# Three constant products instead of seven, block 1 turned by VectorE and DMA instead of TensorE, and a new order of issue, in an adaLN block with linear attention and an MLP

## The chip, the core and the metric

The kernel runs on one core of a Trainium2 chip. A core has a matrix engine (TensorE, PE in the profile, with its weight loads as PEld), VectorE (DVE), ScalarE (ACT), GpSimd (POOL) and SyncE (SP, which here issues every DMA). Each engine takes its instructions strictly in the order in which the program issues them to it; engines wait for each other through semaphores. TensorE writes to PSUM, which has eight banks of 128 x 512 float32.

The metric is the device time of one execution in microseconds (us). Before the change it is 470.25, the median of three runs (469.98 to 470.39).

## What is computed

One token block of 2048 rows and 512 columns goes through an attention half and an MLP half, both modulated by a conditioning vector `c`:

```python
mod = (silu(c) @ w_mod).reshape(1, 6, 1, 512)          # sa, ca, ga, sb, cb, gb
h = layernorm(x) * (1 + ca) + sa
x = x + ga * A(h)                                      # linear attention
h = layernorm(x) * (1 + cb) + sb
x = x + gb * (gelu(layernorm(h) @ w1 + b1) @ w2 + b2)  # 512 -> 1376 -> 512

def A(h):                                              # 32 heads of 16
    q, k, v = split(h @ wqkv)
    pq, pk = q @ w_phi, k @ w_phi                      # per head, 16 x 16
    phi_q, phi_k = [concat(softmax(p), softmax(-p)) for p in (pq, pk)]
    kv, z = phi_k.T @ v, sum(phi_k)
    return (phi_q @ kv / (phi_q @ z + 1e-6)) @ wo
```

All arrays are float32.

## The kernel before

**Numbers and products.** A product of two float32 matrices is made of three products in a rounded format: each operand is split into a high part (a copy on ACT) and a low part (a subtraction on VectorE or POOL), and `mm3` (line 286) multiplies high by high, high by low and low by high. A tile of 128 rows against a 512 x 512 weight is therefore 12 products of 128x128 by 128x512.

**Phases.** The 2048 rows are eight blocks of 256, each with two tiles of 128 rows.

1. *Start.* `w_phi` is folded into the q and k weights: `fold_mm` (line 490) multiplies each of the four row pieces of `wqT` and `wkT` by a block-diagonal matrix `bd`, and `fold_out` splits the result into `wq` and `wk`. The modulation needs silu(c) spread over rows (`silu`, `silu_rows`, the scp products); `mod_cols` (line 372) reduces four loaded pieces `wm` against it to the columns of ca and sa, one piece for each 128 columns of x. `mod_rows` does the other four vectors later, piece by piece, in the background (`bg`, tile `wms`). Seven products of `ones` with itself (tile `warm`, lines 325 to 331) go to TensorE and are never read: four as item `init`, and one each as items `w2`, `w3` and `w4`.
2. *Blocks 0 to 7.* For each block: load x (tile `xt`), row statistics (`ln1_stats`, which ends in a small power on POOL, `rsa`), normalise in place (`ln1_apply`), turn the rows into columns, apply ca and sa (tile `hf`), split (`h_finish`, tile `hT`), then project: pk, pv and pq, each one tile of 12 products for each 128 rows. `k_chain` makes phi_k (on VectorE, ACT and POOL), `kv_mm` accumulates kv over all blocks. The q projections of blocks 3 to 7 are held back (`HOLD`) and fill TensorE later.
3. *The turn.* z and kv are summed up (`z_total`, `kv_blocks`) and the attention of blocks 0 and 1 is finished: t, o, w, la, lb, lc and y in the item names.
4. *Four MLP passes*, 0 to 3, each of 512 rows: `up` (u) and `down` (d), eleven column pieces each, between them the attention of the next two blocks, and the stores of the output (`mlp_out`).

**Turning rows into columns.** There are two ways in `ln1_apply` and `h_transpose`. For a block below `NT` (2 before, so blocks 0 and 1) TensorE transposes eight 128x128 pieces into PSUM (tile `hp`). For the others VectorE transposes 32x32 pieces into a tile `nb`, four DMAs store it to `nt_dram` in short pieces, and one DMA loads it back as `hd` with columns on the partitions. For block 0 `h_first` applies ca and sa and splits piece by piece, and `proj_first` runs its two pk tiles piece by piece (items `pf`), since its weights and modulation come in pieces too. The later blocks go through `hf`.

**The order of issue.** `Later` (line 220) collects every instruction of the program under an item and an engine, and `issue` (line 237) hands them out in the order of the lists in `ISSUE` (line 87), twelve parts: part 0 is the start and block 0, parts 1 to 6 are blocks 1 to 6, part 7 is block 7 and the turn, parts 8 to 11 are the four MLP passes. A word such as `fk.p` is the next instruction, or run of products, of item `fk` on TensorE (p; a is ACT, v VectorE, g POOL, s SP). A plus or minus in front takes it from a later or an earlier part. Item names: `db` loads the small constants, `x` an x block two ahead of the part's own, `dk`, `dq`, `dm`, `dv` the pieces of `wkT`, `wqT`, `wm` and `wv`; `fk`, `fq` fold, `ok`, `oq` split what was folded; `si`, `sr` are silu; `m` in part 0 is `mod_cols`; `s` and `n` are the statistics and the normalising with the turn (`s0`, `s1`, `n0`, `n1` those of blocks 0 and 1), `h` and `f` the way to `hT`; `vs` splits wv; `pk`, `pv`, `q` are projections, `k`, `v` the chains behind them, and `m0` to `m3` from part 1 on the kv products.

**Buffers.** Most tiles of the working set lie in 19 equal buffers; `SLOTS["buf"]` (line 46) names one for each tile in the order in which the program makes them, `SLOTS["bank"]` does so for the PSUM banks, and the other strings for small tiles. A tile waits for the last reader of what lay there before.

Of the kernel before, what the change touches and what calls it, by code (L numbers as in the profile page):

```python
# [15 lines left out]
P = 128  # L16
# [31 lines left out]
    "32eg91ai750d4gf6cf8ehcd187ga30203dh540b52ca0i999hba44571a6i7b8gag3fii0729f4c2fe569d1ehch8d61bg59801c"  # L48
    "7bda51ii68d72i6cc6g44bh676i1ia4e7ah24igi3g908053d78d90d850883efef7g7bbd7b5d5edbfe4id3f8g6f302hbab1ca"
    "gc1d035356268688c6ac633e1e6c0d3h2dffgahfi9f5df3d02gg340052aa2h0f05gc7532d6ggcbhd8g",  # L50
    "bank":
    "3534201077650761644611400766431302014372076341621740122107154521543753631407720101023324531207674567"
    "54567546767640763123523132153152524724605130311550313053514273015015610",
    "st6a": "11101010",
    "sta": "00010101",
    "vea": "01101101",
    "rsa": "01110001",
    "nma": "10111111",
    "dz": "001110010",
    "mxk": "1010101110101010",  # L60
    "smk": "0110010111011011",
    "rck": "1010010111101101",
    "mxq": "10110010",
    "smq": "00000000",
    "rcq": "10100020",
    "den": "00101110",
    "rd": "10111011",
    "st6b0": "10100110",
    "stb0": "10111101",
    "veb0": "10010101",  # L70
    "rsb0": "11001011",
    "st6c0": "01000110",
    "stc0": "10111100",
    "vec0": "00100100",
    "rsc0": "00101000",
    "nmc0": "10010111",
    "st6b1": "11110101",
    "stb1": "10000110",
    "veb1": "11111110",
    "rsb1": "00010101",  # L80
    "st6c1": "10000001",
    "stc1": "10111010",
    "vec1": "00110110",
    "rsc1": "00100101",
    "nmc1": "00000111",
# [3 lines left out]
-init.v -init.p dq.s db.s x0.s dk.s x1.s dk.s dm.s dk.s dm.s si.a bd.v dq.s fq.p s0.v -w2.p oq.a s0.v -w3.p si.v  # L89
-init.v s0.v dk.s s0.v si.v fk.p si.v s0.v dm.s s0.v oq.v s0.g sr.p s1.v n0.v n0.v s1.v n0.a fq.p s1.v n0.v ok.a  # L90
sr.a fk.p s1.v ok.v x.s m.g dm.s m.v h0.p dv.s ok.a fk.p s1.v bg.s s1.v m.v oq.a ok.v m.a m.g m.v h0.p ok.a -w4.p
f.v +x.s s1.g ok.v fq.p m.a n1.v f.a m.v fk.p n1.a f.v dv.s n1.v f.v m.g oq.a pf.p oq.v f.a n1.a f.v ++x.s m.v ok.a
pf.p m.a m.v oq.v m.g f.v h.p s.v f.a fq.p h.a m.v m.a h.p f.v pf.p bg.s h.a s.v +bg.s h.a s.v +bg.s s.v oq.a s.v
m.v s.v f.v s.g +++x.s oq.v f.a bg.g vs.a f.v q1.p n.v +s.v h.a ok.v vs.a n.v vs.v pf.p n.a vs.g ++s.v n.a q0.p k1.v
bg.a n.v n.v +bg.g bg.v n.s pv0.p +s.v n.s f.a +bg.g ++s.v q1.a n.s +bg.a +s.v ++s.v n.s k1.v f.g +bg.a +bg.s ++s.v
++s.v +s.v +s.v ++s.v k0.v f.a pv1.p k0.v f.g +++s.v n.s k1.v ++++x.s +bg.g +s.v k0.v k0.v
""",
    """
pk1.p s.g +s.g n.v n.v bg.v n.a bg.g -k1.v n.a bg.s ++++x.s ++s.v -q0.a +bg.s pk0.p bg.v -k1.a e.v h.a h.a ++s.v
++s.v n.v -k0.a q1.p +n.v bg.v -v1.a +bg.g ++s.v n.v bg.a e.v h.a n.s +n.a n.s -k0.v f.a pv0.p n.s -v0.a f.g n.s h.a  # L100
+bg.v f.a +++s.v e.g bg.a bg.v q0.p f.g k0.v +n.v +n.v +n.a e.g ++++s.v +bg.a +++s.v q1.a +bg.s
""",
    """
q0.p --k1.v -q0.a -n.s +s.v bg.v +s.g n.v bg.g --k0.v n.s -pv1.p -k1.v n.s --k1.v n.s +n.v e.v bg.g n.s -k1.v -e.g
pk0.p h.a --v1.v ++s.v bg.v h.a -e.g +n.v -k1.v bg.a --v0.v ++s.v --k0.g f.a -v1.v -k0.v h.a +++s.v q1.p -v1.a n.s
--v0.v -k0.v +n.a --v1.v --k1.g -k1.v bg.a -k0.v q0.a k0.v h.a pv0.p f.g -k1.a ++s.v bg.v -e.a -k1.v +n.a -m0.p f.a
-m1.p +n.v bg.p pk1.p k0.v bg.a -k0.a bg.s +++s.v ++s.v +n.v ++s.g +h.a v0.v f.g +n.s ++n.v v0.a -k1.v -k0.v +h.a
bg.s pv1.p +n.s -e.a e.g bg.s ++n.v e.v +h.a bg.s +n.s ++n.a +++s.v e.g bg.s +f.a +n.s v1.v
""",
    """  # L110
pk0.p h.a -k1.v --k1.g -bg.s -q1.a ++s.v ++s.v -k0.v +n.a -k1.v -v1.a --v0.v -k0.v -e.g pk1.p k0.v f.g -v0.v --v1.v
--k0.v --v0.v +n.v ++s.g +n.v --k0.g k0.v pv0.p +n.s ++n.v k0.v +n.s ++n.a k0.v +n.s f.a -e.g --e.v -q1.s -k0.a +n.s
# [25 lines left out]
o10.v la00.v o11.v +a0.g -bg.a la00.v la00.v la00.g w11.p +a0.g la01.v +a0.g w1.g lb00.v la01.a +a0.v la01.v lb00.v
w10.p la11.v w1.s q1.s la01.v lb00.v la11.a la01.v la01.v +lp1.s la01.g w2.s la11.v -bg.g lb01.v q3.p la11.v lb01.v
la10.v +a0.g lb01.v la11.v la10.a lb00.v lb01.v la11.v lb00.g lb01.g q3.p la10.v la11.g lc00.v la10.v lc01.v la10.v  # L140
lc01.a la10.v la10.g lb11.v +a0.g lc00.a lb10.v q3.a y0.p q3.a lb11.v y0.p y0.a +a0.g lb10.v q3.s y0.a y0.v --bg.a
lb10.v y0.v
""",
    """
u0.p -w1.a -lb11.v -lb10.v -lb11.v a0.v -lb10.g -lb11.g u0.p a0.v ---bg.g -lc10.v -lc11.v a0.v a0.s -lc10.a a1.v
a0.s u0.p -lc11.a a0.s a1.v a0.s a1.g -y1.p -y1.p -y1.a u0.p --v0.v a0.v a1.g -y1.a -y1.v a0.s a1.g -y1.v a1.a a0.s
u1.p a0.s a1.g a0.s u1.p -w1.g +lp0.s u.a u.a u1.p u.a u.v a0.s u.a a1.v a0.s -w2.g d.p -w1.s u.a d.p u.v u.a d.p
u.v d.p a1.g a1.a d.p d.p -w2.a a1.v d.p a1.g d.p a1.v d.p x0.s a1.v u1.p -w2.g a1.v o01.p o00.p +a0.v d.p o00.a
a1.g -w2.s o01.a o00.v d.p a1.g a1.g +a0.g u.p a1.v o01.v u.a a1.g a1.g d.p a1.g w01.p a1.v u.a +a0.v u.a -w1.a u.v
u.a -w2.g a1.v d.p la01.v a1.s d.p a1.v la01.a a1.s w00.p u.v +a0.g -w2.a a1.s a1.v a1.s -w2.g la01.v a1.s a1.s  # L150
+a0.a u.p a1.s la00.v a1.s la00.a -w1.g -w2.s la00.v la01.v +a0.g la01.v la00.v la00.v la00.v d.p u.a la01.g la01.v
a1.s d.p u.a a1.s +a0.g d.p u.v u.p lb01.v la00.g +a0.a lb00.v -w2.g lb01.v lb00.v lb00.v d.p lb01.v u.a lb01.v
lb00.v lb01.g d.p -w2.a lb00.g lc01.v u.p lc00.v +a0.v lc01.a -w2.g u.a lc00.a u.v y0.v d.p +a0.g u.a y0.v -w2.s
x1.s o10.p +a0.v -w2.s o11.p y0.s u.a d.p y0.s o10.a +a0.g o11.a y0.s d.p o10.v y0.s o11.v w10.p +a0.v +a0.v +a0.v
# [42 lines left out]
u.a u.a d.p u.a u.a u.a u.v d.p d.p d.p d.p d.p out.v d.p out.s d.p out.v d.p out.s d.p out.v d.p out.s out.v out.v  # L197
out.s out.s
""",
]  # L200
W2A = 6
AHEAD = 4
NT = 2
BUFS = 19
ALIGN = 64
NE = 2


class Held:
# [35 lines left out]
def adaln_hedgehog_mixer(ctx, tc, x, wqT, wkT, wv, wo, w1, w2, b2, wmodT, small_in, out):  # L245
    nc = Later(tc.nc)
# [52 lines left out]
    ones = consts.tile([P, 1], F32, name="ones")  # L299
# [16 lines left out]
    bd = wtile("bd", [4, 8, DH])  # L316
# [855 lines left out]
```

## Time and profile before

| | us |
|---|---|
| median of three runs | 470.25 |
| the profiled execution | 470.68 |
| its span in the profile, first to last instruction | 468.9 |
| TensorE busy | 462.5 |
| VectorE, ACT, POOL busy | 314.1, 235.6, 279.7 |

All times in the views count from the start of the span. "Busy" is the union of an engine's instructions; neighbouring instructions overlap at their ends by a little, so the price of a product is the distance between starts, not the duration of one. In the timeline a row stands for a run of like instructions (its start, its length, engine, source line, operation, output and inputs, shape, count). Every line reads L217 or the like, because `Later` issues all instructions from one place; a group is known by its tile names. The granted clock is 0.999 of full speed over the execution.

### The profile page before, as it was taken

Reading aid. Unit: us, or ns where it says so; the run is one execution under the profiler, and the core shown is the slowest. Engines: PE = TensorE matmul, PEld = TensorE weight load, DVE = VectorE, ACT = ScalarE, POOL = GpSimd, SP = SyncE. Lnnn points to the kernel's source line nnn. Section 1 sums busy time; section 2 is a strip of 40 time slices with the busy share of each in tenths; the row PEclk is TensorE's granted clock in tenths of the full one; section 3 lists DMA queues with packets and bytes.
Section 4 is the critical chain, followed back from the end, with each engine's and each line's share of the span. In section 5 each row is a group of like instructions: output and inputs, shape, how many; then the busy total and the mean of one; then the engine's idle time right before and its main releaser. Section 6 shows DMA issues by size and latency. Waiting matters only on the chain.

```text
span 468.9 us, 8567 instructions
## 1 busy us (share of the span) xinstructions
PE 462.5 (99%) x3313; PEld 375.2 (80%) x3313; DVE 314.1 (67%) x610; ACT 235.6 (50%) x383; POOL 279.7 (60%) x233
## 2 busy tenths in 40 slices
PE   9999999999999999999999999999999999999996
PEld 5888888888878878988787878788788788788884
DVE  4999989998848389578885869795873282211113
ACT  2777686855541555758537672166533224422221
POOL 0485859879899989999879975663740010400000
PEclk9999999999999999999999999999999999999999
DMA  8999639636622446937636838168337205100002
GB/s 293 401 263 296 148 78 244 220 65 217 205 64 89 141 174 228 223 112 163 191 97 135 223 113 202 48 110 196 118 76 178 87 0 135 46 22 24 0 1 89
DMA packets 81033, 67.00 MB, mean 143 GB/s; under 512 B 52560, under 2 KB 68320, under 8 KB 80736
## 3 DMA queue, kind: packets, MB, share of 16 engines
q1 hardware_dynamic: 80992, 66.46, 50.1%
q8 instruction: 26, 0.43, 0.4%
q14 instruction: 15, 0.12, 0.1%
HBM read 44.41 MB, written 22.03 MB: 142 GB/s over the span
## 4 chain that ended last, share of the span: by engine, by line
PE 92%; DVE 3%; issue 1%; ACT 1%; DMA 1%; DVEq 0%; ACTq 0%
PE pg L217 26%; PE py L217 26%; PE pv L217 9%; PE pk L217 9%; PE pq L217 7%; PE pw L217 7%; PE warm L217 2%; PE pkv L217 2%; PE fold L217 1%; DVE pw L217 1%; PE po L217 1%; DMA pq_dram<-qs 1%; ACT qT L217 1%; DVE st6c L217 1%; PE zp L217 0%
## 5 line engine op out<-in xcount | busy, mean ns | idle before, releaser
L217 PE MATMUL pg<-yT,w 128*128 128x512 f32 (+1 forms) x528 | 115.5, 370 | 0.7 <-DVE yT L217 0.4
L217 PEld LDWEIGHTS pg<-yT,w 128*128 128x128 f32 x528 | 92.9, 188 | 18.2 <-DVE yT L217 0.6
L217 ACT ACTIVATE pg<-pg,blob 128x512 f32<-128x512 f32 x44 | 29.1, 661 | 106.5 <-PE pg L217 104.3
L217 DVE TENSOR_TENSOR g<-pg,g 128x512 fp32r<-128x512 f32 x40 | 27.2, 684 | 66.9 <-ACT g L217 66.7
L217 PE MATMUL py<-w2a,g 128*128 128x512 f32 x288 | 71.9, 392 | 0.0
L217 PEld LDWEIGHTS py<-w2a,g 128*128 128x128 f32 x288 | 53.5, 188 | 13.4 <-issue 1.6
L217 PE MATMUL py<-w2b,g 128*128 128x512 f32 x192 | 47.2, 390 | 0.0
L217 PE MATMUL pv<-wvh,hT 128*128 128x512 f32 x192 | 45.8, 392 | 0.0
L217 PE MATMUL pk<-wk,hT 128*128 128x512 f32 x192 | 45.6, 391 | 0.0
L217 PE MATMUL pw<-wo,oT 128*128 128x512 f32 x192 | 45.6, 390 | 0.0
L217 PE MATMUL pq<-wq,hT 128*128 128x512 f32 x192 | 45.2, 390 | 0.0
L217 POOL TENSOR_TENSOR ez<-eq,zb 128x1024 f32<-128x1024 f32 x15 | 36.4, 2440 | 13.2 <-PE pg L217 6.1
L217 PEld LDWEIGHTS py<-w2b,g 128*128 128x128 f32 x192 | 35.9, 188 | 8.1 <-issue 0.7
L217 PEld LDWEIGHTS pw<-wo,oT 128*128 128x128 f32 x192 | 35.9, 188 | 7.8 <-issue 0.4
L217 PEld LDWEIGHTS pq<-wq,hT 128*128 128x128 f32 x192 | 35.9, 188 | 7.4
L217 PEld LDWEIGHTS pv<-wvh,hT 128*128 128x128 f32 x192 | 35.7, 188 | 7.5
L217 PEld LDWEIGHTS pk<-wk,hT 128*128 128x128 f32 x192 | 35.8, 188 | 7.3
L217 POOL TENSOR_TENSOR ek<-ek,rck 128x1024 f32<-128x1024 f32 x16 | 31.0, 1947 | 4.3 <-ACT vf L217 1.6
L217 POOL TENSOR_TENSOR eq<-eq,rcq 128x1024 f32<-128x1024 f32 x15 | 28.9, 1939 | 0.2
L217 ACT ACTIVATE g<-pg 128x512 fp32r<-128x512 f32 x40 | 24.0, 599 | 9.5 <-DVE stc L217 2.8
L217 POOL TENSOR_TENSOR rsb<-veb,mhalf 128x1 f32<-128x1 f32 x16 | 8.8, 550 | 30.3 <-DVE veb L217 30.3
L217 POOL TENSOR_TENSOR yT<-yf,yT 128x256 fp32r<-128x256 f32 x24 | 17.1, 744 | 15.2 <-ACT yT L217 15.2
(154 smaller groups left out, 802.4 us busy)
## 6 DMA issues: line engine op xcount, KB each, us to landing
et_dram<-eb SPq DMA_DIRECT2D x48, 128.0 KB, 2.8
eT<-et_dram SPq DMA_DIRECT2D x12, 512.0 KB, 5.5
xt<-in_x SPq DMA_DIRECT2D x8, 512.0 KB, 6.4
wms<-in_wmodT SPq DMA_DIRECT2D x8, 512.0 KB, 5.9
x<-in_x SPq DMA_DIRECT2D x8, 512.0 KB, 3.8
out<-x SPq DMA_DIRECT2D x15, 256.0 KB, 2.1
nt_dram<-nb SPq DMA_DIRECT2D x24, 128.0 KB, 3.3
hd<-nt_dram SPq DMA_DIRECT2D x6, 512.0 KB, 4.2
```

The source lines that it names most:

```text
L217: return lambda *a, **k: self.later.hold(self.letter, lambda: f(*a, **k))
```

## The change

The numbers of `ISSUE` and `SLOTS` are all new. Beside them two things are edited: the constant products are three, all in item `init`, and `NT` is 1, so that block 1 takes the way over `nb`, `nt_dram` and `hd`.

```diff
-    for name in ("init", "w2", "w3", "w4"):
-        nc.item(name)
-        for _ in range(4 if name == "init" else 1):
-            nc.tensor.matmul(warm, ones.to_broadcast([P, P]), ones.to_broadcast([P, 512]), start=True, stop=True)
-    nc.item("init")
+    for _ in range(3):
+        nc.tensor.matmul(warm, ones.to_broadcast([P, P]), ones.to_broadcast([P, 512]), start=True, stop=True)
...
-NT = 2
+NT = 1
...
 ISSUE = [
     """
--init.v -init.p dq.s db.s x0.s dk.s x1.s dk.s dm.s dk.s dm.s si.a bd.v dq.s fq.p s0.v -w2.p oq.a s0.v -w3.p si.v
--init.v s0.v dk.s s0.v si.v fk.p si.v s0.v dm.s s0.v oq.v s0.g sr.p s1.v n0.v n0.v s1.v n0.a fq.p s1.v n0.v ok.a
...
+-init.v -init.v -init.p db.s x0.s x1.s dk.s dq.s dm.s si.a si.v dk.s si.v bd.v si.v dk.s sr.p dq.s s0.v s0.v s0.v
+s0.v s0.v s0.v s0.g sr.a dm.s s1.v s1.v s1.v n0.v s1.v n0.v dm.s s1.v s1.v n0.v s1.g fk.p dm.s ok.a x.s fq.p n0.a
+ok.v fq.p oq.a n1.v n1.v m.v m.g n1.a h0.p dk.s oq.v fk.p m.v m.a n1.v ++x.s fk.p oq.a f.v ok.a oq.v fq.p n1.a ok.v
+fq.p f.a m.g m.v f.v h0.p m.v pf.p n1.v m.a m.g n1.s oq.a f.v ok.a dv.s m.v m.g f.a n1.s m.a f.v pf.p n1.s m.v m.v
+oq.a n1.s m.a f.v dv.s fk.p m.v ok.v f.a bg.s f.v +x.s pf.p oq.v f.v s.v f.a ok.a f.v vs.a oq.v q0.p s.v s.v s.v s.v
+ok.v n1.s q1.p bg.s s.v ++s.v s.g +bg.s vs.a vs.v vs.g n.v ++s.v n.a n.v pf.p n.a n.v n.v pv1.p bg.g ++s.v k0.v n.s
+h.a q0.a +s.v n.s h.a +s.v n.s q1.a +bg.g +s.v ++s.v n.s ++s.v k0.v f.a pv0.p ++++x.s h.a +bg.v f.g +bg.s h.a +s.v
+++s.v k0.v f.a +bg.s +s.v ++s.v +bg.s k1.v +s.g k1.v f.g
...
```

What the lists mean for one engine is seen best by taking its words alone. SP in part 0 (the first `n` four times are a block's stores, the fifth is its load `hd`; an @ and a number marks words of another part):

```text
before  dq db x0 dk x1 dk dm dk dm dq dk dm x dm dv bg x@1 dv x@2 bg bg@1 bg@1 x@3 n n n n bg@1 n x@4
after   db x0 x1 dk dq dm dk dk dq dm dm dm x dk x@2 n1 dv n1 n1 n1 dv bg x@1 n1 bg bg@1 n n n n x@4 bg@1 bg@1 bg@1
```

TensorE in parts 0 to 7, to the turn (the lists go on with t, o, w, q and y):

```text
before  0 init fq w2 w3 fk sr fq fk h0 fk h0 w4 fq fk pf pf h fq h pf q1 pf q0 pv0 pv1
        1 pk1 pk0 q1 pv0 q0
        2 q0 pv1@1 pk0 q1 pv0 m0@1 m1@1 bg pk1 pv1
        3 pk0 pk1 pv0
        4 pk1 pk0 m0@2 m1@2 m0@3 pv1@3 pv1
        5 pk0 pk1 pv0@4 m1@3 m0@4 m1@4 pv0 pv1
        6 pk1 pk0 m0@5 m1@5 m0 pv1
        7 pk1 pk0 m1@6 m1 pv0@6 pv0 pv1 q1 m0 m2 m3 z kf q0 q1 q2 q2 q0 q4 ...
after   0 init sr fk fq fq h0 fk fk fq fq h0 pf pf fk pf q0 q1 pf pv1 pv0
        1 pk1 pk0 q0 pv1 q1 pv0
        2 pk1 pv0 pv1 pk0 q1 m0@1 m1@1 bg q0
        3 pk1 pk0
        4 pk0 pk1 pv1 m0@2 m1@2 m0@3 pv0@3 pv0 pv1@3
        5 pk1 pk0 m1@3 m0@4 m1@4 pv0
        6 pk1 pk0 pv1@5
        7 pk1 m0@5 m1@5 m0@6 pv1@6 pk0 pv0 m1@6 m1 pv1 pv0@6 q1 m0 m2 m3 z kf q1 q2 q0 q2 q0 q4 ...
```

In parts 8 to 11 the products of `u` and `d` are the same and stand in another order among each other; of the stores and loads, the five of block 5's way back to columns (`y1`) move from part 9 to the start of part 10, and two stores of pass 2 move from the start of part 11 to its end, between those of pass 3.

More of the change, by code (lines that the diff above doesn't have):

```diff
@@ L82 @@
[L82 to L85, printed above, removed]
+    "1264710140570135353253136162435026621304533162143502472521023727652170445605353123554624602715375317"
+    "153573175304761253153253215213576546037217123132712723327513246406462",
+    "st6a": "01110010",
+    "sta": "01010101",
+    "vea": "10101001",
+    "rsa": "01110110",
+    "nma": "10001001",
+    "dz": "001001011",
+    "mxk": "1010100110011010",
+    "smk": "0100011001010101",
+    "rck": "0010011010101001",
@@ new lines @@
+    "mxq": "01011011",
+    "smq": "00000000",
+    "rcq": "02002110",
+    "den": "10000010",
+    "rd": "11010110",
+    "st6b0": "10111000",
+    "stb0": "01010111",
+    "veb0": "01100100",
+    "rsb0": "01110010",
+    "st6c0": "11010100",
+    "stc0": "11001000",
+    "vec0": "00110010",
+    "rsc0": "11011010",
+    "nmc0": "11110010",
+    "st6b1": "11110111",
+    "stb1": "00000011",
+    "veb1": "10111001",
+    "rsb1": "01101110",
+    "st6c1": "11100001",
+    "stc1": "01000010",
+    "vec1": "10100011",
@@ L86 @@
+    "rsc1": "01000111",
+    "nmc1": "11011001",
 }
@@ new lines @@
+n.s f.g -v1.v -v0.v +n.a k0.v k1.v -bg.g k1.v -pv1.p -k1.v n.s k0.v -bg.g +n.v k0.a +n.v
+""",
+    """
+pk1.p -k1.a --k1.v n.s -k0.v n.s --v0.a --k0.g --v1.a n.s ----e.v h.a n.s -bg.a pk0.p ----e.s --k1.g -k1.v h.a h.a
+-k0.v f.a n.s k1.v h.a -bg.g -bg.s --m1.p k0.v f.a -m0.p --v0.v -v1.v -m1.p +++lp0.s pv0.p v1.v -k1.v f.g k0.v k1.v
+f.g ----e.v k1.v
+""",
+    """
+pk1.p --k0.g h.a -k1.v -k0.v -k1.a --k1.g h.a -k1.v -v0.a pk0.p ----e.a -k0.v --bg.g f.a k1.v h.a -v0.v k1.v -k0.a
+---v1.v -pv1.p k0.v h.a -k0.v f.g f.a +w1.s --bg.a -k1.v f.g -k0.v --v0.a
@@ new lines @@
+d.p lb10.v d.p lb10.v d.p lb10.v lb11.v d.p lb10.g lb11.v lb11.v lc10.v d.p lb11.g lc10.a +a0.g lc11.v u.p lc11.a
+y1.v u.a y1.v +a1.v y1.s +a0.g y1.s +a1.v u.p u.a y1.s y1.s u.v yf0.a +a1.g yf0.g u.a d.p u.a +a1.g y1.s d.p +a0.v
+u.a d.p u.v yf0.a u.a d.p +a0.v yf0.g u.a u.a d.p ++a0.v u.a xb.g +a0.s d.p +a0.s yf0.a +a0.v yf0.a d.p +a0.s u.a
+u.v +a0.s d.p yf1.a +a0.v yf0.g yf1.a d.p yf1.a +a0.s yf0.g yf1.a d.p d.p +a0.s yf1.g d.p out.v d.p yf1.g +a1.a
+out.v d.p out.s yf1.g out.s +a1.v yf1.g
@@ new lines @@
+""",
+    """
+u.p a0.s a0.s a1.g -out.v a1.g u.p u.a a1.g u.a a0.s u.v a0.s x0.s -out.s a1.a d.p d.p a1.v a1.g d.p d.p u.a u.p u.a
+u.v a1.v a1.v d.p u.a a1.v d.p o00.p -out.v o01.p a1.g a1.g -out.s d.p o00.a a1.g +a0.g a1.v u.a d.p o01.a u.v a1.g
+u.p a1.g o01.v o00.v a1.g a1.v d.p u.a +a0.v d.p u.a w00.p a1.v +a0.g a1.v a1.s +a0.g +a0.a a1.s a1.s +a0.g w01.p
+a1.s la00.v +a0.a a1.v +a0.v a1.s a1.s la00.v d.p a1.s la00.v d.p a1.s +a0.v +lp1.s u.p x1.s la00.v u.v la00.v
+la01.v la00.g a1.s +a0.v a1.s +a0.g d.p u.a la00.v d.p u.a lb00.v d.p lb00.v +a0.g u.p u.v +a0.v la01.v d.p +a1.v
@@ new lines @@
+lb11.v u.a lb11.v u.a lb11.v lb11.v +a0.s lb11.g u.v +a0.s d.p xb.g u.a lb10.v lc11.v +a1.v d.p d.p lb10.v u.p
+lb10.g +a1.g lc10.v +a1.v u.a u.v d.p u.a y0.s d.p lc10.a d.p lc11.a y1.v d.p u.a y1.v u.a
+""",
+    """
+o01.p a1.v -y1.s -u.a -u.a o00.p -u.a -y1.s a1.g a1.v -d.p -y1.s -yf0.a -d.p -y1.s -yf0.a o01.a -d.p x0.s o00.a -d.p
+-u.a o00.v -d.p -u.v -y1.s -yf0.a -d.p o01.v a1.v -d.p -d.p -d.p -out.v -d.p a1.g -d.p -yf0.g -out.v -out.s w01.p
+-out.v a1.g -out.s a1.g -yf0.g a1.v -yf1.a -out.v -yf0.g -yf1.a -yf1.a -yf1.g -yf0.a w00.p -yf1.a -yf1.g -yf1.g a1.g
@@ new lines @@
+-yf1.g -yf0.g u.p a1.g a1.g u.p u.a u.a u.v la00.v a1.v d.p u.a la01.v u.p u.a la01.v a1.v u.v a1.s la01.v a1.s d.p
+u.a a1.v -out.s d.p u.a a1.s la01.v la01.v la01.v d.p la01.g -out.s la00.v a1.s d.p lb01.v d.p la00.v d.p la00.v
+a1.v u.p u.v a1.s la00.v lb01.v a1.s la00.g la00.v a1.s a1.s lb00.v d.p u.a lb01.v d.p u.a d.p u.v d.p lb00.v a1.s
+d.p lb00.v lb00.v lb01.v lb00.g d.p a1.s lb01.g lc00.v d.p lc01.v u.p u.p u.a lc00.a u.a lc01.a u.v y0.v d.p u.a
+y0.v o11.p u.a o10.p y0.s y0.s d.p o10.a o11.a y0.s o10.v d.p x1.s o11.v d.p y0.s d.p w10.p w11.p la10.v u.v y0.s
@@ new lines @@
+""",
+    """
+u.p u.p u.a u.a u.v -out.v -out.v d.p -out.s u.a d.p -out.s u.a -d.p d.p -out.v d.p u.v d.p u.p u.p u.a u.a u.v d.p
+u.a d.p u.a d.p u.v d.p d.p d.p d.p d.p d.p d.p d.p u.p -d.p u.a u.p -out.v u.a u.v d.p u.a d.p u.a d.p u.v d.p d.p
+u.p d.p u.a d.p u.a d.p u.v u.p d.p u.a d.p u.a d.p u.v d.p d.p d.p d.p u.p d.p u.a u.p u.a u.v u.p u.a u.a u.v d.p
+u.a d.p u.a d.p u.a u.a d.p u.a u.a u.a u.v d.p d.p d.p d.p out.v d.p out.s d.p out.v -out.s -out.s d.p out.s d.p
+out.v d.p out.s out.v out.v out.s out.s
```

172 lines of the change are left out of this document (54 added, 118 removed).

## Prediction

> **What bounds the kernel now.** I read the page's busy line and its chain of work first: is one engine the bound?
>
> ```profile
> PE 462.5 (99%) x3313; PEld 375.2 (80%) x3313; DVE 314.1 (67%) x610; ACT 235.6 (50%) x383; POOL 279.7 (60%) x233
> PE 92%; DVE 3%; issue 1%; ACT 1%; DMA 1%; DVEq 0%; ACTq 0%
> ```
>
> TensorE is busy 462.5 of 468.9 us, and 92% of the chain lies on it. Next I read what it waited for; these are all of its waits but the 0.9 us before its first product:
>
> ```profile
> PE zp L217 <- ACT kvT L217: 0.5, 1, 0.5
> PE pg L217 <- DVE yT L217: 0.4, 1, 0.4
> PE po L217 <- ACT qT L217: 0.4, 1, 0.4
> PE pg L217 <- ACT yT L217: 0.3, 1, 0.3
> ```
>
> Only 1.6 us in all. So there are two ways to a shorter time: take work off TensorE, or lose those waits. Any new wait of TensorE counts in full. Third, its timeline at the start, where the change takes work away (start, duration, operation):
>
> ```profile
> 0.92 6.67 PE L217 MATMUL warm<-ones 128*128 128x512 f32 x8 [0.92 <-DVE ones L217]
> 7.43 1.05 PE L217 MATMUL fold<-bd,q 128*128 128x128 f32 x8
> 8.31 1.89 PE L217 MATMUL warm<-ones 128*128 128x512 f32 x4
> 10.04 1.05 PE L217 MATMUL fold<-bd,k 128*128 128x128 f32 x8
> ...
> 15.68 1.03 PE L217 MATMUL warm<-ones 128*128 128x512 f32 x2
> 16.55 1.05 PE L217 MATMUL fold<-bd,q 128*128 128x128 f32 x8
> ...
> 21.09 0.60 PE L217 MATMUL hp<-blob,xt 128*128 128x128 f32 x4
> 21.52 1.06 PE L217 MATMUL fold<-bd,q 128*128 128x128 f32 x8
> 22.41 0.60 PE L217 MATMUL hp<-blob,xt 128*128 128x128 f32 x4
> ...
> 31.03 5.60 PE L217 MATMUL pv<-wvh,hT 128*128 128x512 f32 x24
> 36.47 5.60 PE L217 MATMUL pk<-wk,hT 128*128 128x512 f32 x24
> ```
>
> **What is removed.** Prices are differences of starts. w2 and w3: 10.04 - 8.31 = 1.73 us. w4: 16.55 - 15.68 = 0.87. Block 1's transposes through TensorE (the hp rows at 21.09 and 22.41): 21.52 - 21.09 = 0.43, twice, 0.86. The fourth product at the very start: a quarter of 7.43 - 0.92 = 6.51, so 1.63. Sum: **5.1 us** of TensorE work. That is a ceiling, since the products may only have filled a wait for data.
>
> **What is late next: the loads.** The new order of SP puts the fourth piece of wk (dk) behind three pieces of the modulation weights and x of block 2, the wv loads (dv) behind x of block 4 and block 1's four stores, and block 1's load hd behind those. So I work out landings from the rate of the transfers (the columns are the stretch, its length, busy time of TensorE, its weight loads, VectorE, ACT and POOL, the granted clock, the DMA's busy share, GB/s):
>
> ```profile
> 0.00:10.00 10.00, 9.08 (x20) 4.37 (x21) 3.47 (x14) 2.09 (x3) 0.91 (x5) 1.00 0.84 272
> 10.00:20.00 10.00, 9.91 (x75) 8.90 (x74) 8.94 (x29) 8.01 (x17) 5.43 (x5) 1.00 1.03 405
> 20.00:30.00 10.00, 10.00 (x54) 8.53 (x53) 9.59 (x24) 7.91 (x17) 5.19 (x4) 1.00 0.99 380
> 32.00:34.00 2.00, 2.00 (x11) 1.65 (x10) 2.00 (x11) 2.00 (x6) 2.00 (x2) 1.00 1.03 174
> ```
>
> The engines of the DMA are full from 10 to 30 us, so landing goes by bytes in the queue: 2.72 MB by 10 us, then 0.405 MB/us, from 20 us 0.38. A test on before: the last k piece, with 4.30 MB up to and with it, is served at 10 + 1.58/0.405 = 13.9; it landed at 6.81 + 8.2 = 15.0:
>
> ```profile
> 6.81 0.33 SPq L217 DMA_DIRECT2D k<-in_wkT  x1
> k<-in_wkT SPq DMA_DIRECT2D x1, 256.0 KB, 8.2
> ```
>
> So I add 1.1 us. Block 1's stores to nt_dram go in short pieces; while block 2's ran (last row of the windows) a full queue moved 174 GB/s in place of 380 to 405, so they count double. In the new order:
> - last k piece: 5.88 MB, 10 + 3.16/0.405 + 1.1 = **18.9** (before 15.0);
> - second half of wv: 8.50 MB counted; 6.77 are through by 20, so 20 + 1.73/0.38 + 1.1 = **25.7**;
> - hd of block 1: 10.07 MB, 20 + 3.30/0.38 + 1.1 = **29.8**.
>
> **TensorE's new start, gate by gate.** Three products end near 6.0. Silu's rows, seven folds, block 0's transposes and two of the four groups of the first pk (pf) follow as pieces land. The second of these groups wants the second modulation piece, which is at 4.04 MB: 10 + 1.32/0.405 + 1.1 = 14.4. Four or five VectorE steps of some 0.6 us (the transposes' row further down shows such a step) bring its rows to about 17.0, and a group takes 1.36 (a quarter of 36.47 - 31.03 = 5.44, for half as many products as a tile of 2.72), so 18.4; TensorE then waits 0.5 for the last k piece. From 18.9: one fold (8.31 - 7.43 = 0.9), pf 1.36, q0 and q1 2.72 each, pf 1.36: 9.1, so v starts at **28.0** against 31.03. Gate two: wv's second half needs a copy on ACT and a subtraction on POOL:
>
> ```profile
> 25.90 1.09 ACT L217 ACTIVATE wvh<-wv_s 128x1024 fp32r<-128x1024 f32 x1
> 27.06 3.19 POOL L217 TENSOR_TENSOR wvh<-wv_s,wvh 128x1024 fp32r<-128x1024 f32 x1 [1.52 <-ACT wvh L217]
> ```
>
> 25.7 + 1.0 + 3.2 = 29.9, needed 1.36 + 0.45 after v starts, at 29.8: a wait of 0.1 to 0.2. Two v tiles (5.44) end at **33.6**. Gate three: block 1's transposed rows.
>
> ```profile
> L217 ACT ACTIVATE hf<-hd,affine x8: 585/592/601, 40.4 to 59.4; 128x256 f32<-128x256 f32 x8
> L217 ACT ACTIVATE hT<-hf x5: 614/624/633, 31.1 to 56.1; 128x512 fp32r<-128x512 f32 x5
> L217 POOL TENSOR_TENSOR hT<-hf,hT x4: 1297/1301/1319, 32.7 to 47.6; 128x512 fp32r<-128x512 f32 x4
> ```
>
> From 29.8 ACT does hf, a q copy, hf, a q copy and the first hT: some 0.5 us apart, 32.0; POOL's 1.3 ends at 33.3. Two more hf, hT, and POOL with a small rs in between: 35.3. Wanted at 33.6 + 0.45 and 33.6 + 1.36 + 0.45 = 35.4. So all three gates nearly tie, and pk of block 1 starts at 33.6 against 36.47: **2.9 us earlier**; 2.2 of the 5.1 turn into waits for loads.
>
> **What is added beside it.** Two VectorE transposes (0.70 each), four stores and one load. VectorE has room where they fall, before 26 us, and none just after:
>
> ```profile
> L217 DVE STREAM_TRANSPOSE nb<-xt x12: 652/700/712, 29.1 to 99.6; 128x512 f32<-128x512 f32 x12
> 0.00:26.00 26.00, 24.99 (x128) 18.51 (x129) 18.00 (x58) 15.02 (x32) 8.59 (x12) 1.00 0.96 351
> 26.00:60.00 34.00, 34.00 (x151) 28.16 (x151) 33.14 (x83) 23.85 (x49) 26.24 (x21) 1.00 0.79 224
> ```
>
> I take 0; with that cover gone, VectorE's 1.4 us come late and cost up to 1.4. The second transpose waits on VectorE behind the reduction of the second modulation piece (about 14.4), so it ends near 16.4. SP stands at block 1's first store until then, with both wv loads queued behind; the transfers still have work until 20.3 (x of block 4 is the last in the queue), so I take 0 and keep 0 to 1.5. The fewer constant products cost nothing by themselves: at the start they run 1.63 each, later 0.87, so the array speeds up between; silu's rows keep it busy across that point (I keep 0 to 0.9, the folds at half pace, which lies ahead of the 18.9 gate).
>
> By the Trainium skill, "DMA: Bandwidth & Descriptors", Specifications, transfers in pieces under 512 B cost a read-modify-write, which speaks against a further block through DRAM in the fullest part of the queue; the 174 GB/s window agrees, and the sum above already pays it from that row. Were short pieces free, hd and the second half of wv would land 1.4 us sooner (0.52/0.38) and the sum would gain the 0.2 of the v gate; at a third of the rate it is rival B.
>
> **The rest of the order.** From 36.47 on the products are the same in number and kind; I take the 1.6 us of waits as they were (the same items stand around zp, po and the first pg in the new lists), and 0.3 for new small waits, between -1.6 and the rival below. At the end two stores of pass 2 go between the last ones on SP; they drain before the last product, so 0. Sum: 2.9 - 0.3 = **2.6 us**. The profiled execution took 470.68 (span 468.9 and 1.8 around it), so 468.1 there; against the median of 470.25: **467.6**.
>
> **Rivals.**
> (A) *A later block's rows come late, slower.* The new order defers v and m tiles, so block 7's first pk stands further ahead than the gain alone puts it. I add up the new list from 33.6 (26 tiles of 2.72 and eight kv tiles of 0.6, a third of the pkv row below, are 75.5): it starts at 109.1, where 117.5 - 2.9 would be 114.6. Before, and VectorE's busy time around it:
>
> ```profile
> 105.32 0.38 SPq L217 DMA_DIRECT2D hd<-nt_dram  x1
> 114.14 2.57 POOL L217 TENSOR_TENSOR hT<-hf,hT 128x512 fp32r<-128x512 f32 x2
> 112.88 1.85 PE L217 MATMUL pkv<-ek,vf 128*17 128x32 f32 x192
> 117.50 2.88 PE L217 MATMUL pk<-wk,hT 128*128 128x512 f32 x12
> 60.00:90.00 30.00, 30.00 (x439) 24.70 (x439) 26.81 (x56) 21.73 (x35) 23.96 (x18) 1.00 0.58 158
> 90.00:123.00 33.00, 33.00 (x513) 27.09 (x511) 30.12 (x55) 19.34 (x28) 28.53 (x17) 1.00 0.61 184
> ```
>
> From hd's issue to the end of hT: 116.7 - 105.3 = 11.4. The second half of hT is wanted 1.8 into the tile, at 110.9, so hd must be issued by 99.5. On SP it waits behind block 7's four stores, these on VectorE's transposes, and VectorE, full until 60, may be behind. If the chain keeps before's time, hT is done at 116.7, 5.8 late: 470.25 - 2.6 + 5.8 = **473.4**. It decides from 2.6 us late. For it: the tile is pulled 5.5 us beyond the gain. Against: VectorE waits 3.2 + 2.9 us between 60 and 123, and before ran its own tight order there without a wait of TensorE.
> (B) *The hd gate is late.* The stores share a full queue; if they are served at a third of the rate (1.4 us more) and SP stands 0.6 longer, hd lands 2 us later and pk of block 1 waits 2: **469.6**, no measurable change.
> (C) *The products were filler.* If the last k piece lands at 21 (SP held up by a buffer), everything from 28.0 shifts by 2.1: **469.7**. It would mean that the change does not do what it says: work goes, waits come.
> (D) *The remaining waits go too.* Loads 1 us sooner and half of the 1.6 us gone: about **465.7**.
>
> **How the numbers follow.** Forecast 0.62 (467.6; its own range 466.3 to 469.2), A 0.19, B 0.08, C 0.06, D 0.05. A measurement here tells a change from none at about 0.2%, 0.94 us. Faster: 0.62 + 0.05 = 0.67; the same: B and C, 0.14; slower: A, 0.19. The range takes D in below and the nearer part of A above: 465.3 to 471.3.
>
> **What would show it.** Right: 6 and not 14 passes of warm; no hp of block 1; pk's first row x24 of block 1 near 33.6; the last k piece landing near 19, hd near 30; TensorE idle some 2 us more in the first 20 us and busy throughout from 34 to 130. Wrong: a wait of TensorE on hT of POOL or ACT between 35 and 120 (A), a wait there of over 1 us just before 34 (B), TensorE idle over 2 us ahead of the last fold (C), or pass 2's products of pg waiting for yf, whose stores moved into the next part.

## The result, and the profile after

| | us |
|---|---|
| before, median of 12 runs | 470.21 (469.42 to 470.56) |
| after, median of 12 runs | 467.74 (466.95 to 469.86) |
| ratio, 95% interval | 0.9949 (0.9937 to 0.996) |
| after, the profiled execution and its span | 468.37, 466.6 |

The changed kernel is 2.5 us faster. Its runs spread over 2.9 us, those of before over 1.1. First the busy line of the page of the changed kernel:

```profile
PE 458.5 (98%) x3297; PEld 372.3 (80%) x3297; DVE 317.1 (68%) x612; ACT 234.6 (50%) x381; POOL 279.7 (60%) x233
```

TensorE's busy time fell by 4.0 us and the span by 2.3, so 1.7 us of what went came back as idle time. (By the starts 5.1 us were priced as removed; a busy row also holds short gaps between its instructions, so the two need not agree.) These are all waits of TensorE after (in total, times, longest):

```profile
PE warm L218 <- DVE mhalf L218: 0.9, 1, 0.9
PE fold L218 <- DMA k<-in_wkT: 0.9, 1, 0.9
PE pk L218 <- ACT hT L218: 0.7, 1, 0.7
PE zp L218 <- ACT kvT L218: 0.6, 1, 0.6
PE pg L218 <- DVE yT L218: 0.3, 1, 0.3
PE pg L218 <- ACT yT L218: 0.3, 1, 0.3
PE po L218 <- DMA eT<-et_dram: 0.2, 1, 0.2
PE pk L218 <- POOL hT L218: 0.2, 1, 0.2
```

The timeline of TensorE at the start shows where the first three fall (start, duration, operation, wait before it):

```profile
0.92 5.11 PE L218 MATMUL warm<-ones 128*128 128x512 f32 x6 [0.92 <-DVE mhalf L218]
5.86 1.05 PE L218 MATMUL scp<-blob,sc 128*128 128x128 f32 x8
7.78 1.16 PE L218 MATMUL fold<-bd,k 128*128 128x128 f32 x8 [0.86 <-DMA k<-in_wkT]
...
15.32 1.64 PE L218 MATMUL pk<-wk,hT 128*128 128x512 f32 x6
17.63 1.65 PE L218 MATMUL pk<-wk,hT 128*128 128x512 f32 x6 [0.68 <-ACT hT L218]
19.12 1.05 PE L218 MATMUL fold<-bd,k 128*128 128x128 f32 x8
...
28.20 5.60 PE L218 MATMUL pv<-wvh,hT 128*128 128x512 f32 x24
33.64 2.02 PE L218 MATMUL pk<-wk,hT 128*128 128x512 f32 x8
35.82 3.94 PE L218 MATMUL pk<-wk,hT 128*128 128x512 f32 x16 [0.17 <-POOL hT L218]
39.60 0.62 PE L218 MATMUL pq<-wq,hT 128*128 128x512 f32 x2
```

Block 1's pk starts at 33.64 against 36.47, and takes 39.60 - 33.64 = 5.96 where two tiles cost 5.44. Of the 5.1 us that went, 2.3 are lost ahead of it: 1.54 in the two waits listed (0.86 and 0.68), the rest in gaps that the list does not have (the fold at 7.78 is followed at 9.06, 1.28 later, where one costs 0.89). From there on I follow the gain by the starts of the same mark in both kernels. Before and after, in that order, the marks are the last q tile ahead of the turn, the first and the second run of pw, and the last row:

```profile
132.53 2.88 PE L217 MATMUL pq<-wq,hT 128*128 128x512 f32 x12
...
163.53 3.01 PE L217 MATMUL pw<-wo,oT 128*128 128x512 f32 x12
166.93 1.58 PE L217 MATMUL po<-qT,gab 64*32 64x256 f32 x32 [0.39 <-ACT qT L217]
168.44 8.46 PE L217 MATMUL pw<-wo,oT 128*128 128x512 f32 x36
...
459.82 0.51 PE L217 MATMUL py<-last,last 32*128 32x512 f32 x4
...
464.52 0.62 PE L217 MATMUL py<-wlast,glast 128*128 128x512 f32 x2
```

The same marks in the changed kernel:

```profile
130.47 2.88 PE L218 MATMUL pq<-wq,hT 128*128 128x512 f32 x12
...
161.39 3.00 PE L218 MATMUL pw<-wo,oT 128*128 128x512 f32 x12
...
165.34 8.45 PE L218 MATMUL pw<-wo,oT 128*128 128x512 f32 x36
...
456.83 1.00 PE L218 MATMUL py<-last,last 32*128 32x512 f32 x4
...
462.07 0.63 PE L218 MATMUL py<-wlast,glast 128*128 128x512 f32 x2
```

The gain is 2.83 us at block 1's pk, 2.06 at the last q tile, 2.14 at the first pw, 3.10 at the second (the wait of po for qT is gone; whether the change removed it is asked below), and 2.45 at the last row. Half a microsecond of it is lost in the last pass: the four products on the last rows take 1.00 in place of 0.51. Behind the last row 466.6 - 462.07 = 4.53 remain, before 468.9 - 464.52 = 4.38.

### The profile page after: what moved, and what is told of

Same layout as the page of the kernel before. It is cut to its first block, busy times and chain, and to the rows that moved or that the text cites. A ratio compares the mean times of both kernels' runs of the same rounds, so it can differ in the third digit from the quotient of the medians.

```text
span 466.6 us, 8536 instructions
## 1 busy us (share of the span) xinstructions
PE 458.5 (98%) x3297; PEld 372.3 (80%) x3297; DVE 317.1 (68%) x612; ACT 234.6 (50%) x381; POOL 279.7 (60%) x233
## 4 chain that ended last, share of the span: by engine, by line
PE 85%; DMA 5%; DVE 4%; POOL 2%; issue 1%; ACT 1%; SPq 0%; DVEq 0%; POOLq 0%; ACTq 0%
PE py L218 25%; PE pg L218 24%; PE pv L218 8%; PE pk L218 8%; PE pw L218 8%; PE pq L218 7%; PE pkv L218 2%; DMA wm<-in_wmodT 2%; PE po L218 1%; DVE pw L218 1%; DMA eT<-et_dram 1%; DMA wms<-in_wmodT 1%; DMA xt<-in_x 1%; PE qp L218 1%; POOL w2a L218 1%
## 5 line engine op out<-in xcount | busy, mean ns | idle before, releaser
L218 PE MATMUL py<-w2a,g 128*128 128x512 f32 x288 | 70.7, 391 | 0.0
L218 DVE TENSOR_REDUCE smq<-eq 128x64 f32<-128x1024 f32 x16 | 19.2, 1207 | 6.8 <-ACT eq L218 6.8
```

The lines of the kernel that those rows point to most:

```text
L218: return lambda *a, **k: self.later.hold(self.letter, lambda: f(*a, **k))
```

## Experiments

Theory: the gain is made ahead of block 1's pk; the products that went were partly cover for loads, so undoing one part gives back less than its price, and what waits there is the second modulation piece. Rivals: the prices of the removed work add up; or the order alone makes the gain and the products were filler. All ratios are to the kernel before, run on the same chip.

**The changed kernel again.**

> The changed kernel unchanged, for comparison on the same chip. Expected 467.7 (467.0 to 469.9, the spread of its first runs).

Measured 467.95 (467.18 to 468.03), ratio 0.995 (0.9938 to 0.9961). The same.

**Three products in the old order.**

```diff
-    for name in ("init", "w2", "w3", "w4"):
+    for name in ("init",):
...
-        for _ in range(4 if name == "init" else 1):
+        for _ in range(3):
...
--w2.p -w3.p -w4.p (in part 0 of ISSUE)
```

> The kernel before with three constant products in place of seven, all in the first item, and nothing else changed. Theory (the loads are late next): 4.2 us of products go, but the list of loads is that of before, so most of it turns into waits for the pieces of wk, wq and the modulation: 0.8 to 2.5 us faster than before, likeliest 1.3 (468.9). Rival 1 (prices add up): 4.2 faster, 466.0. Rival 2 (all of the gain comes from the new order, the products were filler): no change, 470.2.

Measured 469.61, ratio 0.9989 (0.9979 to 0.9999): 0.8 us by the medians and 0.5 by the ratio, at the lower end of the theory's range or under it. 3.4 of the 4.2 us do not arrive. The timeline shows two of the waits that came in their place, and two marks further on:

```profile
7.74 1.16 PE L213 MATMUL fold<-bd,k 128*128 128x128 f32 x8 [0.37 <-DMA k<-in_wkT]
...
13.76 0.66 PE L213 MATMUL hp<-blob,xt 128*128 128x128 f32 x4 [0.61 <-DVE wk L213]
...
162.23 3.01 PE L213 MATMUL pw<-wo,oT 128*128 128x512 f32 x12
...
166.20 8.71 PE L213 MATMUL pw<-wo,oT 128*128 128x512 f32 x36
...
180.91 1.09 PE L213 MATMUL yp<-blob,h 128*128 128x128 f32 x8 [0.56 <-ACT h L213]
```

The first is a load; in the second the transposes wait for VectorE to empty the PSUM bank of a k fold. This profile is 1.41 us ahead of before at block 1's pk (35.06), 2.24 at the second pw, and 1.27 at yp, which waits there for ACT's h. So the old order loses twice: to the loads at the start, and at yp.

**Seven products in the new order.**

```diff
-    for _ in range(3):
+    for name in ("init", "w2", "w3", "w4"):
+      nc.item(name)
+      for _ in range(4 if name == "init" else 1):
...
-sr.p ... fk.p ... h0.p ... h0.p ... pf.p
+sr.p ... fk.p -w2.p -w3.p ... h0.p ... h0.p -w4.p ... pf.p
```

> The changed kernel with seven constant products again: four at the start, two behind the first fold, one behind the second transpose of block 0 (the constant tile lies in another PSUM bank for this). Theory (the second modulation piece gates the second group of the first pk at 17.6, and TensorE has some 2.4 us of waits ahead of it): 1.2 to 2.0 us slower than the changed kernel, likeliest 1.6 (469.3). Rival (prices add up): 4.1 slower, 471.8. Rival (filler): no change, 467.7.

Measured 469.68, ratio 0.9987 (0.9978 to 0.9996): 1.7 us over the repeat of the changed kernel. The theory's number; neither 4.1 nor 0. Its wait on hT ahead of the second pf group is gone. So the new order with all products is worth some 0.8 us, the fewer products in the old order 0.8, and both together 2.5. Where the two help each other is shown only in part. At block 1's pk the gains are 0.60 (new order alone, 35.87), 1.41 (fewer products alone) and 2.83 (both), but these are single executions: with the old start unchanged, the profile with the other qT buffer, next, has this pk at 35.58, 0.89 ahead of before. Clearer is yp. There the old order with three products gives back 1.0 us of its lead, the new order nothing (3.10 at the second pw and at yp), and in no profile of the new order does yp wait. Which of the many moves of the new order do it was not tried.

**The buffer of one qT tile, in the kernel before.**

```diff
 SLOTS["buf"][130]
-4
+e
```

> The kernel before with one letter of the buffer list changed: the second qT tile of block 1 lies in a buffer that is not being stored to DRAM at that time, so that its copy on ACT does not wait for that store. Theory (the 0.96 us that the changed kernel gains between the first and the third pw is this wait): 0.9 us faster than before, 469.3. Rival (VectorE's chain behind it sets the time of the next products anyway): no change, 470.2.

Measured 469.86, ratio 0.9992 (0.9983 to 1.0): no change that can be told. Its timeline:

```profile
162.66 3.01 PE L215 MATMUL pw<-wo,oT 128*128 128x512 f32 x12
...
166.62 8.60 PE L215 MATMUL pw<-wo,oT 128*128 128x512 f32 x36
...
181.24 1.09 PE L215 MATMUL yp<-blob,h 128*128 128x128 f32 x8 [0.57 <-ACT h L215]
```

From the first to the second pw it takes 3.96 where before takes 4.91, so the wait is not there. But that is not shown to be the edit's work: the kernel with three products, whose buffers are those of before, takes 3.97 over the same stretch. The store that the copy of qT waits for landed 4.6 us after its issue in the profile of before and 3.5 in both others, by the view of DMA issues (before, then three products):

```profile
pq_dram<-qs SPq DMA_DIRECT2D x1, 512.0 KB, 4.6
...
pq_dram<-qs SPq DMA_DIRECT2D x1, 512.0 KB, 3.5
```

Whether the wait comes in other executions of before is open. What both profiles do show is the rival. Yp, which ran at 182.18 before without a wait, waits 0.57 and 0.56 for ACT's h, at the end of VectorE's chain of statistics, and what was gained at po is given back by the next yp: this profile's lead, which came with 0.87 from a quicker start, is 1.82 at the second pw and 0.78 there. So the rival holds for the old order. In the changed kernel h is done at 178.1, yp starts at 179.08 with no wait, and the 0.96 stays.

**Block 1 by TensorE again.**

```diff
-NT = 1
+NT = 2
...
-n1.v n1.v n1.s n1.s n1.s n1.s n1.s
-... fk.p m.v ok.v ... q1.p bg.s
+... fk.p h.p m.v ok.v ... q1.p h.p bg.s
...
-bg.a (last of part 1)      --bg.v (in part 2)
+-bg.a, -bg.v (first bg of part 1)
```

> The changed kernel with block 1 turned by TensorE again: its eight transposes behind the last k fold and behind the second q tile, its two VectorE transposes, four stores and one load gone; for a buffer, two background steps of one modulation piece come earlier. Theory: 0.86 us of TensorE work comes back and the 0.3 to 0.5 us in which pk of block 1 waited for its rows goes: 0.3 to 0.9 us slower than the changed kernel, likeliest 0.5 (468.2). Rival 1 (the way over DRAM was what loaded the queue and ACT, and everything behind lands sooner without it): 0.5 or more faster, 467.2. Rival 2 (the work adds up and the wait stays): 0.9 to 1.2 slower.

(The lists of buffers and banks lose or gain the letters of the tiles that go or come; one more letter differs.) Measured 467.96 (467.58 to 468.35), ratio 0.9959 (0.9946 to 0.9972), beside 0.995 for the repeat of the changed kernel: between no change and the theory's 0.5. Block 1's pk starts 0.7 later, and both its tiles run through:

```profile
34.34 5.60 PE L212 MATMUL pk<-wk,hT 128*128 128x512 f32 x24
39.78 0.39 PE L212 MATMUL pq<-wq,hT 128*128 128x512 f32 x1
```

The q tile behind starts at 39.78 against 39.60. Most of the 0.86 us of transposes that the change removed came back as the 0.5 that pk waits for its rows over DRAM. In the repeat of the changed kernel hd landed at 29.0 in place of 29.8 and pk has no such wait. At the turn the three profiles are level: zp starts at 135.66 (changed), 135.64 (repeat) and 135.68 (this one). By the ratios the edit alone is worth 0.4 us, by the medians nothing; the intervals cannot tell.

**One product.**

```diff
-    for _ in range(3):
+    for _ in range(1):
```

> The changed kernel with one constant product in place of three. Theory (the gates at 7.8, 14.3 and 17.6 absorb what goes, and the array comes to full pace by the folds' own work): 0 to 0.3 us slower or faster, no change, 467.8. Rival 1 (three products' time is on the path): 1.6 or more faster, 466.0. Rival 2 (the array stays at half pace over the folds without them): 1 to 2 slower, 469.2, with fold rows of 8 passes that take about twice their 0.9 us.

Measured 470.49 (469.79 to 471.85), ratio 1.0014 (1.0005 to 1.0023): 2.5 us slower than the changed kernel by the medians and 3.0 by the ratios, beyond both theory and rival 2. Rival 2 saw the folds right:

```profile
4.13 2.07 PE L218 MATMUL scp<-blob,sc 128*128 128x128 f32 x8 [1.14 <-DVE sc L218]
7.59 2.07 PE L218 MATMUL fold<-bd,k 128*128 128x128 f32 x8 [1.38 <-DMA k<-in_wkT]
9.45 2.85 PE L218 MATMUL fold<-bd,q 128*128 128x128 f32 x16
```

Eight passes take 2.07 where the changed kernel's take 1.05 and 1.16. But that cost is absorbed by the gates, as the theory said: block 1's pk starts at 33.86, 0.22 later. What is lost is lost far behind, in the last kv products ahead of the turn:

```profile
133.83 1.08 PE L218 MATMUL pkv<-ek,vf 128*17 128x32 f32 x107
136.60 0.93 PE L218 MATMUL pkv<-ek,vf 128*17 128x32 f32 x85 [1.69 <-issue]
```

"issue" means that TensorE waited for nothing that the profile shows. No other profile here has such a stop of TensorE; the last experiment asks about it.

**The last wk piece earlier.**

```diff
-... x.s ... h0.p dk.s oq.v
+... dk.s x.s ... h0.p oq.v
```

> The changed kernel with the last piece of wk loaded ahead of x of block 2. The prediction's claim (TensorE waits for that piece, 18.9): 0.3 to 0.5 us faster, 467.3. What the trace of the changed kernel says (the wait at 17.6 is for the rows of block 0 by the second modulation piece, and the fold behind it starts at once at 19.1, 0.3 after the piece has landed): no change, 467.7.

Measured 467.46 (467.08 to 470.0), ratio 0.9958 (0.9944 to 0.9973). The piece, by the view of DMA issues 8.6 us on the way from 8.76, lands at 17.4 in place of 18.8, and TensorE still waits at the same place for as long:

```profile
17.55 1.65 PE L215 MATMUL pk<-wk,hT 128*128 128x512 f32 x6 [0.69 <-ACT hT L215]
```

No change: the gate is the modulation piece, not the wk piece.

**Block 1's stores earlier.**

```diff
-... m.v m.v ... pf.p n1.v m.a
+... m.v n1.v m.v ... pf.p m.a
-... ++x.s ... dv.s ... dv.s
+... dv.s ... dv.s ++x.s
-... s.v ++s.v s.g ... ++s.v n.a n.v ... n.v n.v pv1.p
+... s.v s.g ... n.a n.v ... n.v n.v ++s.v ++s.v pv1.p
```

> The changed kernel with block 1's second VectorE transpose ahead of the reduction of the second modulation piece, x of block 4 behind the second load of wv, and the first statistics of block 3 (two VectorE steps) behind block 2's transposes. Theory (pk of block 1 loses 0.3 to 0.5 us to late rows, since its stores and hd queue behind those): hd lands 1 us or more sooner, the wait on POOL's hT ahead of 36 goes, 0.3 to 0.6 us faster, 467.3. Rival (the modulation piece's reduction, 0.6 later, moves the wait at 17.6 by as much): 0.3 to 0.6 slower, 468.2.

Measured 468.24 (467.64 to 468.82), ratio 0.9967 (0.9955 to 0.9979): no gain. Block 1's pk starts 0.5 sooner, at 33.11, its second part still waits 0.17 for POOL, and the lead is spent in the first MLP pass, where the second half of po waits 0.56 for eT from DRAM (0.2 after):

```profile
199.80 0.67 PE L215 MATMUL po<-eT,gab 64*32 64x256 f32 x16 [0.56 <-DMA eT<-et_dram]
```

**The last pass, three times.** Before, the d products between the last u and the products on the last rows were 15 passes, after 12. In the first two kernels the d ahead of the last three u is moved behind the last of them; in the third it is the d behind the first of these three. All three also issue pass 2's late stores early; the second and third load the wk piece early as well.

```diff
-d.p u.p d.p u.a u.p u.a u.v u.p u.a u.a u.v d.p u.a d.p u.a d.p u.a u.a d.p
+u.p d.p u.a u.p u.a u.v u.p u.a u.a u.v d.p u.a d.p u.a d.p u.a u.a d.p d.p
...
+d.p u.p u.a u.p u.a u.v u.p u.a u.a u.v d.p u.a d.p u.a d.p u.a u.a d.p d.p
```

> The changed kernel with two edits in the last part alone: five d products instead of four stand behind the last u (one is moved from ahead of the last two u), and the two stores of pass 2 that stood between those of pass 3 are issued before pass 3's own. Theory (the four products on the last rows wait 0.45 us for ACT's last copies, and the two late stores lengthen the end by 0.15): 0.4 to 0.7 us faster than the changed kernel, likeliest 0.6 (467.2), with the row of the last rows' four products at 0.5 in place of 1.00. Rival (the moved product only lets the wait fall ahead of the two u's own copies): no change, 467.8.

> The changed kernel with the last piece of wk ahead of x of block 2, and with both edits of the last part (five d products behind the last u, pass 2's two late stores before pass 3's). If the two are independent: 0.7 to 1.2 us faster than the changed kernel, likeliest 0.9 (466.9), and faster than both kernels. Rival (what is gained ahead of block 1 is given back at the later waits for VectorE and loads): that of the last part alone, 467.2.

> The changed kernel with the last piece of wk ahead of x of block 2, pass 2's two late stores before pass 3's, and five d products behind the last u by another choice: the one moved is the first of a tile of g, which stood between the last two u, not the last of a tile as in the two kernels before, where ACT waited for that tile's buffer. Theory (0.45 us of wait for ACT's last copies and 0.15 at the stores go): from the last u's start to the end 0.6 us less than in the changed kernel, four products on the last rows in 0.5 in place of 1.00, no wait of py on ACT; 467.0 (466.6 to 467.6), faster than both kernels. Rival (the three u without a product between them wait for a bank or for ACT): 467.7 or more.

Measured 469.25 (ratio 0.9986, 0.9977 to 0.9995), 469.18 (0.9978, 0.9969 to 0.9987) and 469.37 (0.999, 0.9979 to 1.0001): 1.3 to 1.5 us slower than the changed kernel by the medians, 1.3 to 1.9 by the ratios. All three have the same waits in the last pass. The first one's timeline, ACT and TensorE:

```profile
453.79 0.84 PE L215 MATMUL py<-w2b,g 128*128 128x512 f32 x3
454.71 0.60 ACT L215 ACTIVATE g<-pg 128x512 fp32r<-128x512 f32 x1 [6.18 <-PE py L215]
...
455.36 3.28 PE L215 MATMUL py<-w2b,g 128*128 128x512 f32 x12 [0.74 <-ACT g L215]
...
458.68 1.38 PE L215 MATMUL py<-last,last 32*128 32x512 f32 x4
```

ACT's copy of the next g stands until one d product has run, 453.79 to 454.6: by this wait, that d is the last reader of the g tile whose buffer the copy takes. It had run ahead of the last two u; behind them it holds ACT and all copies that follow. The d run in a fixed sequence, so the first and the third choice put the same d behind the last u, and the guess written down for the third, that it was the first of a tile, was wrong. The stores' part is as expected: 468.6 - 464.23 = 4.4 behind the last row, 0.1 to 0.2 less than after. The wait for ACT's last copies was not removed by any of them, and none of the kernels tried is faster than the changed one by more than can be told.

**One product and two short ones.**

```diff
-    for _ in range(3):
-        nc.tensor.matmul(warm, ones.to_broadcast([P, P]), ones.to_broadcast([P, 512]), start=True, stop=True)
+    for n in (512, 32, 32):
+        nc.tensor.matmul(warm[:, :n], ones.to_broadcast([P, P]), ones.to_broadcast([P, n]), start=True, stop=True)
```

> The changed kernel with one constant product of 512 columns and two of 32, so that TensorE has as many instructions as in the changed kernel, and nearly as little work as with one product. With one product alone TensorE stood 1.69 us within the kv products at 135, waiting for nothing that the profile shows. Theory (that stop comes with the place of the instructions, not with the array's pace): no such stop, 0 to 0.6 us slower than the changed kernel, likeliest 0.3 (468.1). Rival (it comes from the missing work at the start): the stop comes again, 470.4.

Measured 468.71 (468.08 to 469.37), ratio 0.9967 (0.9955 to 0.9979). No stop: the last kv products are one row again.

```profile
133.17 1.82 PE L218 MATMUL pkv<-ek,vf 128*17 128x32 f32 x192
```

Its slowest run is under the fastest one of the kernel with one product, though on another chip, and the medians differ by 1.8 us, about the 1.69 of the stop; so that kernel seems to lose the time in every run and not by chance in one. At the turn this kernel is level with the changed one; behind it po waits twice for eT in pass 0, 0.9 in all (0.2 after), and 0.65 of the loss shows at the pw behind. That the stop goes with two short products, which add instructions and next to no work, speaks for the place of the instructions. How it comes about is not settled, but the views of the DMA queues point at one load of instructions. Queue q8 has 26 such loads in every kernel. With one product the eleventh is served at 134.2 (there is none from 125 to 134, and from 133 to 134 the engines of the DMA are 98% busy with data), and TensorE stops at 134.9. In the changed kernel the eleventh is served at 125.8 and with two short products at 131.5, before the kv products begin; the loads at 135.0 and 134.8 in these two are the twelfth. The number of instructions alone does not set its time: the second kernel of the last pass has as many as the changed one, has its eleventh load at 131.7, and no stop. The Trainium skill, "Runtime: NRT & Kernel Launch", Instruction fetch mechanics, says that instructions come in blocks of 256 by such loads and that their cost is mostly hidden; if the stop is such a load, as its time suggests and no run here proves, a dense run of small products behind a full queue is where it isn't.

## Why the prediction was right, and where it was not

**The size and its place: right.** 2.6 us were forecast, 2.5 measured, from 2.9 at block 1's pk (2.83 between the two profiles). The 2.83 is partly luck: measured from the profile with the other qT buffer, whose start is that of before, it is 1.94, since full pace came late in the profile from which the prices were read. The landings worked out from bytes hold: the last wk piece 18.8 (18.9), hd 23.87 + 5.9 = 29.8 (29.8), the second half of wv 18.93 + 6.0 = 24.9 (25.7). That 2.2 of 5.1 us turn into waits is what the starts show (5.1 - 2.83 = 2.3), and that removed products are worth less than their price is borne out from both sides, by three products in the old order (0.8 of 4.2) and seven in the new (1.7 of 4.1).

**The first gate: wrong cause, right time.** The step "TensorE then waits 0.5 for the last k piece" failed. It waited 0.68 at 17.63 for block 0's rows with the second modulation piece, and the fold at 19.12 began with no wait; the wk piece 1.4 us earlier changed nothing. The second modulation piece was there when the prediction had it (14.2 for 14.4). In the chain behind it the prediction counted VectorE's steps and took the rows as there by 17.0. Its second vector goes over POOL and ACT, and in the changed kernel the chain reads:

```profile
14.30 3.90 POOL L218 TENSOR_TENSOR prod<-wm,cb 128x512 f32<-128x512 f32 x3 [2.56 <-DMA wm<-in_wmodT]
...
15.61 0.63 ACT L218 ACTIVATE prod<-prod 128x512 f32<-128x512 f32 x1 [1.16 <-POOL prod L218]
16.37 0.55 DVE L218 TENSOR_SCALAR hp<-hp,affine 128x256 f32<-128x256 f32 x1 [0.40 <-ACT prod L218]
17.19 0.38 ACT L218 ACTIVATE hT<-hp 128x256 fp32r<-128x256 f32 x1
```

POOL 1.3 (the first of its three), ACT 0.8, VectorE 0.55 and a copy end at 17.6. With the wk piece as the gate the fold would have begun at 18.8; it began at 19.1. The two gates lie 0.3 apart, and only by this luck did the time come out.

**Block 1's transposes: a term that was mis-sized.** 0.86 us were counted as removed. Put back alone they cost 0 to 0.4, since pk then no longer waits for its rows: at the third gate, of those that "nearly tie", the new way loses 0.5 in this execution, where hd landed at 29.8, and nothing in the repeat, where it landed at 29.0. VectorE's extra 1.4 us and SP's standing cost nothing visible, as taken.

**Constant products: right, with a price where none was looked for.** Half pace over the folds, the bound of 0.9, costs 0.22 at block 1's pk with one product. The price of the fourth product, 1.63, was from an execution in which full pace came late; the old start took 5.62 in place of 6.51 in the profile with the other qT buffer, and in the new order four products took 5.40 where three took 4.94.

**The later waits: wrong one by one, right in sum.** "I take the 1.6 us of waits as they were" failed at po: the gain grew there by 0.96. Part or all of that may be a slow store in the one profile of before, as the three products in the old order show; that the new order does not lose it again at yp is shown. Against it stand 0.77 between block 1's pk and the last q tile (0.3 was allowed; 0.5 of it is block 1's wait), and in the last pass 0.5 for ACT's copies, which no step had. The stores at the end cost 0.15, not 0.

**The rivals.** A: block 7's first pk starts with no wait, at 110.64:

```profile
110.64 2.88 PE L218 MATMUL pk<-wk,hT 128*128 128x512 f32 x12
```

B and C did not come: hd and the last wk piece landed as worked out. C's idea, that the products were filler, holds for over half of their price in either order.

## What to carry to other kernels

Price removed work by the gate that is late next, and follow that gate's whole chain over all engines: here the gate named and the one that held lay 0.3 us apart, and moving the first did nothing. A removed wait is worth something only if the next engine in the chain is early too: in the old order what was gained at po was lost again at yp. And before a wait is put down to a cause, look for it in a second profile without the edit. Before a product is moved, ask which buffer it is the last to read: moving one d of 0.68 us cost some 1.4.

## What was not expected of the hardware

Full pace of TensorE came at another time in each execution, and the granted clock column, 1.00 throughout the first 10 us, does not show it; the distance of passes does: 0.86 at first (two passes of the changed kernel take 1.71, from 3.64 to 5.35), then 0.43 (the two of w4, before, take 0.87). With the same start, eight passes took 6.51 (before) and 5.62 (other qT buffer) to the next row; six took 4.45 and 4.94 in two executions of the changed kernel. By this estimate the change of pace lies between 3.7 us (six passes in 4.45: 4.35 slow ones of 0.86) and 6.1 us (eight in 6.51: 7.1 slow ones) after the first product. The Trainium skill, "TensorE: Matmul & The Clock Gate", Part 1, says about 4 us, give or take 0.5, and elsewhere in that part that the window of activity runs freely; the rows here spread as the second says and wider than the first.

With one product full pace came only after 9.45, and the stop of 1.69 us at 135 depended on two products at 1 us. A change at the very start can cost its time more than 100 us later, and the profile lists no engine and no data that TensorE waited for.
